# Batch 0's first-stage results moved inside SBUF, x laid out for 2 KB packets, and seven weight bands begun among batch 0's pairs

## The chip, the cores and the metric

The kernel runs on one core of one Trainium2 chip. The metric is the device time of one execution, in microseconds (us); the time before is 2643.61 us, the median of three runs (2640.65 to 2645.09 us). A profile of one further execution goes with it.

## The reference

`reference` has two halves. The first takes x (8 batches, 3008 positions, 256 channels), does a real FFT along the positions, multiplies each frequency by a complex 256x256 matrix, adds a bias, shrinks both parts towards zero by 0.01, and transforms back. The second is a feed-forward layer on the 24064 rows that result.

```python
X = np.fft.rfft(x, axis=1)
Yr = Xr @ w_r - Xi @ w_i + b_r
Yi = Xr @ w_i + Xi @ w_r + b_i
Yr = np.sign(Yr) * np.maximum(np.abs(Yr) - lam, 0.0)   # Yi likewise, lam = 0.01
y = np.fft.irfft(Y, n=x.shape[1], axis=1)
h = y.reshape(-1, 256) @ moe_w_in        # 256 x 2048, given in float64
g = h * np.clip(h + 3.0, 0.0, 6.0) / 6.0
return g @ moe_w_out                      # 2048 x 256, float64
```

## The kernel before

**The transform.** 3008 is 64 times 47, so a transform of one batch is a transform of length 47 (`stage1`), one of length 64 (`s2` in `middle`), the complex matrix and the shrinking (`s3`), one of length 64 back (`s5`), and one of length 47 back (`segment`). Between them the data change from one arrangement over the partitions to another, and they do so by way of DRAM: `scr1` between `stage1` and `s2`, `scr2` between `s5` and `segment`.

**Stage 1 of batch 0** handles seven sets of the 64 rows n1: one of four rows (96 partitions) and six of ten (120 partitions). For each set and for each of two results (c = 0, 1), TensorE makes one product into PSUM (L295), ScalarE copies it to a tile `a` (L303), and ScalarE's DMA queue stores it to `scr1` (L305, `scr<-a`). A partition of `a` is one pair (n1, k); `s2` wants n1 and c on the partitions and k in the free dimension. So `middle(0)` loads, for each of twelve pairs g of k, 128 partitions x 2 KB of `scr1` (L367, `bt<-scr`) and a piece of the table f64 (L368, `f<-in_f`).

**The pairs of batch 0.** `s2(g)`: eight products (L376); ScalarE and VectorE split the result into a high and a low part, the tile `X` (L130 and L131). `s3(g)`: 24 products of `X` with the matrices (L137, into `ps_a`), then VectorE adds the bias and shrinks (L414, L425, L426), ScalarE multiplies signs (L429), and copies of 64 partitions (`zt<-tc`, DMA L439, or VectorE L437 for the last two pairs) turn the tile. `s5(g)`: two products (L453), a copy (L455), a store to `scr2` (L456). Then two segments are loaded (`qt<-scr`), transformed (L505) and joined (`raw`, L515 and L527), and `prepare(0)` makes the seven split operands `yb` of the first 512 rows.

**The weight bands.** The weights of the second half come as float64. Each is cut into eight bands (`in_band`, `out_band`), and a band is decoded on the chip: one load of 512 KB (L178, `st<-in_w_in` or `st<-in_w_out`); then on VectorE L190, L191, L195, L199; on ScalarE L193, L194, L197; on GpSimd L200 and, for an `in` band, four sums (L217); and then the split into a high part by ScalarE and a low part by VectorE (`w_in_lo`, `w_out_lo`). An `in` band has seven instructions on VectorE (three for the low part), an `out` band five: 96 for all sixteen bands. `turn` begins a band and moves those begun a step on. Among batch 0's pairs it begins one at steps 0, 3, 9, 18 and 27 of 36 (`EARLY`, which uses the buffers `raw` and `yb`); after them and in the main loop it begins the rest (`LATE`, other buffers).

**The main loop** goes through 47 chunks of 512 rows and eight bands each: products with `w_in` (`pb`, `pc`, `pd`, L137), the gate (L608, L610, and a split `gs`), products with `w_out` (L631). The transforms of batches 1 to 7 are laid among them.

**What sets the order.** The code gives an order, and a scheduler moves an instruction ahead when it holds its buffers and inputs to be there. On the chip each engine, and each engine's DMA queue, takes its instructions in the order that results. Every DMA counts on one of eight semaphores, in turn, and waits until the DMA eight before it (the one before on that semaphore) has landed; the queues of SyncE (SP) and ScalarE share the eight.

## Time and profile before

| what | value |
|---|---|
| median of three runs | 2643.61 us |
| profiled execution, its own time | 2643.59 us |
| its span | 2641.8 us |
| TensorE busy | 2562.4 us (97%) |
| VectorE busy | 1975.7 us (75%) |
| ScalarE busy | 1820.1 us (69%) |
| granted TensorE clock, mean | 0.988 |

The span is the time from the first to the last instruction of the profiled execution; the 1.8 us between it and that execution's time lie around it. A busy share is a mean over stages of very different kinds: the first 135 us hold the transform of batch 0 and most of the decoding of weights, and what follows is the main loop. The stages are therefore read from a table of stretches, not from the page's shares.

### The profile page before, as it was taken

How to read it: one execution, taken by the hardware profiler on the slowest of the kernel's cores; microseconds unless marked ns; L12 is line 12 of the kernel's file. 1: busy time of each engine (PE TensorE's matmuls, PEld its weight loads, DVE VectorE, ACT ScalarE, POOL GpSimd, SP SyncE). 2: the span in 40 equal slices, each digit the busy share in tenths (PEclk: the TensorE clock that was granted, in tenths of full speed). 3: DMA queues.
4: the chain of work that ended last, by engine and by line, in shares of the span. 5: the costliest groups of instructions: out<-in, count | busy, mean ns of one | idle time of the engine just before them, and what ended most of it. 6: DMA issues, size and time to landing. Idle time of an engine off the chain costs nothing.

```text
span 2641.8 us, 44527 instructions
## 1 busy us (share of the span) xinstructions
PE 2562.4 (97%) x16406; PEld 2291.9 (87%) x16406; DVE 1975.7 (75%) x3186; ACT 1820.1 (69%) x3592; POOL 796.0 (30%) x749
## 2 busy tenths in 40 slices
PE   5789999999999999999999999999999999999999
PEld 3577998988898998988898998999889889898887
DVE  7786886877677777777777777777777777666766
ACT  5476677767667777766776777677777666676766
POOL 2263334443233332233323333233321121121210
PEclk8889999999999999999999999999999999999999
DMA  7623333332223321323213322233221111100000
GB/s 216 191 79 93 103 104 94 113 107 75 59 60 96 88 69 48 85 78 90 73 49 86 88 76 63 76 84 84 63 79 58 50 53 53 43 26 30 12 17 17
DMA packets 150178, 199.98 MB, mean 76 GB/s; under 512 B 16847, under 2 KB 104135, under 8 KB 149959
## 3 DMA queue, kind: packets, MB, share of 16 engines
q1 hardware_dynamic: 146675, 193.98, 25.4%
q10 hardware_dynamic: 3284, 3.15, 0.4%
q8 instruction: 129, 2.11, 0.3%
q14 instruction: 90, 0.74, 0.1%
HBM read 97.45 MB, written 74.97 MB: 65 GB/s over the span
## 4 chain that ended last, share of the span: by engine, by line
PE 84%; DVE 4%; ACT 4%; DMA 2%; POOL 2%; issue 2%; SPq 0%; ACTq 0%; POOLq 0%; DVEq 0%
PE po L631 36%; PE pb L137 17%; PE ps_a L137 11%; PE pc L137 9%; PE pd L137 4%; PE ps_a L505 3%; PE ps_a L376 3%; ACT gs L130 1%; DMA xin<-in_x 1%; DVE r L610 1%; ACT r L608 1%; DVE gs L131 1%; POOL e L288 1%; DVE h L572 1%; POOL yb L131 0%
## 5 line engine op out<-in xcount | busy, mean ns | idle before, releaser
L631 PE MATMUL po<-gs,w_out_hi 128*128 128x512 f32 x3008 | 1006.5, 396 | 0.0
L610 DVE SCALAR_TENSOR_TENSOR r<-r,h 128x1024 f32<-128x1024 f32 x376 | 486.9, 1295 | 267.7 <-ACT r L608 265.9
L631 PEld LDWEIGHTS po<-gs,w_out_hi 128*128 128x128 f32 x3008 | 541.3, 188 | 85.5
L631 PE MATMUL po<-gs,w_out_lo 128*128 128x512 f32 x1504 | 601.9, 400 | 5.9 <-ACT gs L130 3.3
L608 ACT ACTIVATE r<-h,three 128x1024 f32<-128x1024 f32 x376 | 434.3, 1155 | 214.6 <-DVE h L572 211.6
L137 PE MATMUL pb<-yb,w_in_hi 128*128 128x256 f32 x3008 | 571.6, 279 | 2.5 <-POOL yb L131 2.5
L131 DVE TENSOR_TENSOR gs<-r,gs 128x1024 fp32r<-128x1024 f32 x376 | 484.4, 1288 | 80.7 <-ACT gs L130 78.8
L137 PEld LDWEIGHTS pb<-yb,w_in_hi 128*128 128x128 f32 x3008 | 461.0, 189 | 22.5 <-POOL yb L131 2.7
L130 ACT CAST gs<-r 128x1024 fp32r<-128x1024 f32 x376 | 395.8, 1053 | 92.5 <-DVE r L610 89.5
L572 DVE TENSOR_TENSOR h<-pc,u 128x256 f32<-128x256 f32 x752 | 315.1, 419 | 175.3 <-PE pc L137 160.1
L131 POOL TENSOR_TENSOR yb<-T,yb 128x256 fp32r<-128x256 f32 x188 | 181.0, 969 | 859.4 <-ACT yb L130 841.6
L137 PE MATMUL pb<-yb,w_in_lo 128*128 128x256 f32 x1504 | 431.3, 288 | 4.6 <-ACT p L567 1.6
L567 ACT COPY u<-pb 128x256 f32<-128x256 f32 x752 | 277.8, 373 | 121.5 <-PE pb L137 103.8
L631 PEld LDWEIGHTS po<-gs,w_out_lo 128*128 128x128 f32 x1504 | 284.0, 189 | 63.3 <-ACT gs L130 14.5
L137 PEld LDWEIGHTS pb<-yb,w_in_lo 128*128 128x128 f32 x1504 | 284.3, 189 | 29.7 <-ACT h L601 4.1
L137 PE MATMUL pc<-yb,w_in_hi 128*128 128x256 f32 x1504 | 297.6, 279 | 0.8 <-POOL yb L131 0.8
L137 PEld LDWEIGHTS pc<-yb,w_in_hi 128*128 128x128 f32 x1504 | 230.7, 189 | 13.3 <-POOL yb L131 1.1
L137 PE MATMUL pc<-yb,w_in_lo 128*128 128x256 f32 x752 | 219.0, 291 | 5.5 <-DVE h L572 4.9
L567 ACT COPY p<-pb 128x256 f32<-128x256 f32 x376 | 139.9, 372 | 80.9 <-PE pb L137 78.6
L601 ACT COPY h<-pb 128x256 f32<-128x256 f32 x376 | 140.5, 374 | 57.4 <-PE pb L137 55.4
L572 DVE TENSOR_TENSOR h<-pd,p 128x256 f32<-128x256 f32 x376 | 156.7, 417 | 14.9 <-ACT p L567 10.2
L137 PEld LDWEIGHTS pc<-yb,w_in_lo 128*128 128x128 f32 x752 | 142.1, 189 | 21.7 <-DVE h L572 7.9
(125 smaller groups left out, 3928.9 us busy)
## 6 DMA issues: line engine op xcount, KB each, us to landing
bt<-scr SPq DMA_DIRECT2D x96, 256.0 KB, 2.9
scr<-pt SPq DMA_DIRECT2D x96, 256.0 KB, 2.4
zt<-tc SPq DMA_DIRECT2D x376, 64.0 KB, 2.0
out<-ot SPq DMA_DIRECT2D x94, 256.0 KB, 2.3
xin<-in_x SPq DMA_DIRECT2D x48, 480.0 KB, 4.8
qt<-scr SPq DMA_DIRECT2D x96, 240.0 KB, 3.5
scr<-a SPq DMA_DIRECT2D x84, 240.0 KB, 2.5
f<-in_f SPq DMA_DIRECT2D x96, 128.0 KB, 2.8
```

The source lines that it names most:

```text
L130: nc.scalar.copy(out=hi, in_=src)
L131: (on or nc.vector).tensor_tensor(out=lo, in0=src, in1=hi.bitcast(F32), op=ALU.subtract)
L137: nc.tensor.matmul(out=ps, lhsT=a, rhs=b, start=start and n == 0, stop=stop and n == len(todo) - 1, skip_group_check=more,)
L288: (nc.vector if b == 0 else nc.gpsimd).tensor_tensor(out=e, in0=plus, in1=minus, op=ALU.add)
L376: nc.tensor.matmul(out=psv[:, dh, :, u, :], lhsT=data[:, u, dh * P : (dh + 1) * P], rhs=f[:, u, :], start=True, stop=True,)
L505: nc.tensor.matmul(out=ps[:, cs * w + g * rows : cs * w + (g + 1) * rows], lhsT=qt[:rows, cs, g, dh * P : (dh + 1) * P], rhs=f47_s[2][:row ...
L567: nc.scalar.copy(out=t, in_=ps)
L572: nc.vector.tensor_tensor(out=to, in0=ps, in1=keep.pop((i, n)), op=ALU.add)
L601: nc.scalar.copy(out=hs[i][:, 1, :H], in_=pb)
L608: nc.scalar.activation(out=r, in_=h, func=AF.Relu, bias=three, scale=1.0)
L610: nc.vector.scalar_tensor_tensor(out=r, in0=r, scalar=6.0, in1=h, op0=ALU.min, op1=ALU.mult)
L631: nc.tensor.matmul(out=pos[dh], lhsT=w[:, ft * D + dh * P : ft * D + (dh + 1) * P], rhs=g[:, low, u], start=f == 0 and u == 0 and which == ...
```

## The change

It has three parts.

1. **Batch 0's stage-1 results stay in SBUF.** The two tiles `w_in_hi` and `w_in_lo` become one tile of sixteen slots: slot f is the high part of band f, and slot 15 - f its low part. Slots 4 to 10 (the high parts of bands 4 to 7 and the low parts of 5 to 7) also serve as `spread`, a view of 24 x 256 floats per partition, until the bands are written there. Instead of a store to `scr1` and twelve loads, each tile `a` is copied by DMA from 120 partitions x 1 KB to five partitions x 24 KB of `spread`, one copy per half of the tile (`g`): the first half by ScalarE's queue, the second by SP's. There are 26 such copies (the small set has one half). `s2` reads `spread` directly; the twelve loads `bt<-scr` of batch 0 are gone. Batches 1 to 7 keep `scr1`.
2. **x is laid out on the host as two rows of sixteen blocks** per partition, so that a load of a set has two runs of 2 KB per partition where it had one of 4 KB (for the small set two of 1 KB for one of 2 KB).
3. **`EARLY` bands** are begun at steps 0, 3, 9, 15, 21, 27 and 33: seven.

```diff
-    win_s = [const.tile([P, nf, 7, P], F32R, name="w_in_" + t) for t in ("hi", "lo")]
+    win_t = const.tile([P, 2 * nf, 7, P], F32R, name="w_in")
+    win_s = [[win_t[:, f] for f in range(nf)], [win_t[:, 2 * nf - 1 - f] for f in range(nf)]]
+    spread = win_t[:, nf // 2 : nf // 2 + 7].rearrange("p f s c -> p (f s c)").bitcast(F32)
+    spread = spread[:, : NK * D].rearrange("p (k d) -> p k d", d=D)
...
-            at = n1 // J * 2 * D
-            src = x[b, :rows, at : at + 2 * w].rearrange("p (s c) -> p s c", s=2)
+            at = n1 // J * D
+            src = x[b, :rows].rearrange("p (s c) -> p s c", s=2)[:, :, at : at + w]
...
-                dst = scr1[b][c, n1 : n1 + n].rearrange("(g j) k d -> (j k) g d", g=w // D)
-                (nc.sync if b else nc.scalar).dma_start(out=dst, in_=a.rearrange("p (g d) -> p g d", d=D))
+                if b:
+                    dst = scr1[b][c, n1 : n1 + n].rearrange("(g j) k d -> (j k) g d", g=w // D)
+                    nc.sync.dma_start(out=dst, in_=a.rearrange("p (g d) -> p g d", d=D))
+                else:
+                    for g in range(w // D):
+                        at = c * N1 + n1 + g * J
+                        queue = nc.sync if g else nc.scalar
+                        queue.dma_start(out=spread[at : at + rows // NK], in_=a[:, g * D : (g + 1) * D])
...
-            bt[g] = space([P, 2, D], F32, "bt"), space([P, 2, P], F32, "f64")
-            nc.sync.dma_start(out=bt[g][0], in_=src[:, 2 * g : 2 * g + 2, :])
+            bt[g] = space([P, 2, D], F32, "bt") if b else spread[:, 2 * g : 2 * g + 2], space([P, 2, P], F32, "f64")
+            if b:
+                nc.sync.dma_start(out=bt[g][0], in_=src[:, 2 * g : 2 * g + 2, :])
...
-            turn(EARLY if i == 3 or i % 9 == 0 else None)
+            turn(EARLY if i == 0 or i % 6 == 3 else None)
```

What this does to the order of the instructions shows at three places. In the rows below, a name is that of a tile with its number mostly left out, `w_in<-a` is a copy into `spread`, and the line numbers after the change are a few higher.

SP's queue at the end of stage 1, where the tables and the first bands are loaded. Before:

```order
L151 DMA g_all<-in_g 128x128
L368 DMA f_232<-in_f 128x256
L368 DMA f_236<-in_f 128x256
L178 DMA st<-in_w_in 128x2x512 x4
L178 DMA st<-in_w_out 128x1024
L367 DMA bt<-scr_95 128x512 x2
```

After:

```order
L151 DMA g_all<-in_g 128x128
L315 DMA w_in<-a 5x24x256 x3
L379 DMA f_241<-in_f 128x256
L315 DMA w_in<-a 5x24x256 x4
L379 DMA f_243<-in_f 128x256
L181 DMA st<-in_w_in 128x2x512
L315 DMA w_in<-a 5x24x256 x2
L181 DMA st<-in_w_in 128x2x512 x2
L181 DMA st<-in_w_out 128x1024 x2
```

Twelve copies into `spread` (nine of them here) now stand in this queue, and ten of the twelve stand ahead of the first band's load.

VectorE up to the split of the first pair (`X<-pb,X`). Before, the last rows ahead of it:

```order
L131 TENSOR_TENSOR w_in_lo<-m,w_in_hi 128x256
L131 TENSOR_TENSOR w_in_lo<-m,w_in_hi 128x128
L195 SCALAR_TENSOR_TENSOR e<-st,e 128x512
L190 TENSOR_SCALAR e<-st 128x512
L191 TENSOR_SCALAR m<-st 128x512
L199 SCALAR_TENSOR_TENSOR m<-m,r 128x512
L131 TENSOR_TENSOR X<-pb,X 128x2x256
```

After, all rows from the first instruction on a band:

```order
L193 TENSOR_SCALAR e<-st 128x512
L194 TENSOR_SCALAR m<-st 128x512
L198 SCALAR_TENSOR_TENSOR e<-st,e 128x512
L202 SCALAR_TENSOR_TENSOR m<-m,r 128x512
L193 TENSOR_SCALAR e<-st 128x512
L194 TENSOR_SCALAR m<-st 128x512
L131 TENSOR_TENSOR X<-pb,X 128x2x256
```

Before, 23 of the 96 band instructions of VectorE stand ahead of this split; after, six.

VectorE among the later pairs, from the seventh split. Before, up to the eighth:

```order
L131 TENSOR_TENSOR X<-pb,X 128x2x256
L414 TENSOR_TENSOR tc<-ps_a,bias 128x512
L425 TENSOR_SCALAR tc<-tc 128x512
L426 TENSOR_TENSOR tc<-tc 128x512
L131 TENSOR_TENSOR X<-pb,X 128x2x256
```

After, where the next row is the eighth split:

```order
L131 TENSOR_TENSOR X<-pb,X 128x2x256
L437 TENSOR_TENSOR tc<-tc 128x512
L198 SCALAR_TENSOR_TENSOR e<-st,e 128x512
L131 TENSOR_TENSOR w_in<-m,w_in 128x256
L131 TENSOR_TENSOR w_in<-m,w_in 128x128
L202 SCALAR_TENSOR_TENSOR m<-m,r 128x512
L425 TENSOR_TENSOR tc<-ps_a,bias 128x512
L131 TENSOR_TENSOR w_in<-e,w_in 128x512
L436 TENSOR_SCALAR tc<-tc 128x512
L437 TENSOR_TENSOR tc<-tc 128x512
L131 TENSOR_TENSOR w_out_lo<-m,w_out_hi 128x512
L425 TENSOR_TENSOR tc<-ps_a,bias 128x512
```

Between the first split and the twelfth and last stand 20 band instructions before and 54 after. From there to the last `zt` copies there are 10 before and 6 after, from these to the first sum of the main loop (`h<-pd`) 28 and 22, and later 15 and 8.

More of the change, by code (lines that the diff above doesn't have):

```diff
@@ L218, in in_band @@
         yield
-        hi, lo = (t[:, f] for t in win_s)
+        hi, lo = (t[f] for t in win_s)
         split(hi[:, :2], lo[:, :2], w[:, :, :P])
@@ L264, in stage1 @@
     def stage1(b):
-        scr1[b] = dram.tile([2, N1, NK, D], F32, name="scr1")
+        if b:
+            scr1[b] = dram.tile([2, N1, NK, D], F32, name="scr1")
         sets = SEGS[-1:] + SEGS[:-1]
@@ L354, in middle @@
         scr2[b] = dram.tile([2, N1, NK, D], F32, name="scr2")
-        src = scr1[b].rearrange("c n k d -> (c n) k d")
+        src = scr1[b].rearrange("c n k d -> (c n) k d") if b else None
         dst = scr2[b].rearrange("c n k d -> (c n) k d")
@@ L365, in load @@
         def load(g):
-            bt[g] = space([P, 2, D], F32, "bt"), space([P, 2, P], F32, "f64")
-            nc.sync.dma_start(out=bt[g][0], in_=src[:, 2 * g : 2 * g + 2, :])
+            bt[g] = space([P, 2, D], F32, "bt") if b else spread[:, 2 * g : 2 * g + 2], space([P, 2, P], F32, "f64")
+            if b:
+                nc.sync.dma_start(out=bt[g][0], in_=src[:, 2 * g : 2 * g + 2, :])
             nc.sync.dma_start(out=bt[g][1], in_=f64.rearrange("p (k c) -> p k c", c=P)[:, 2 * g : 2 * g + 2])
@@ L561, in block @@
         c, f = units[i]
-        product(ps, [(tuple(t[:, f, WEIGHT[n]] for t in win_s), yb[c, n])], start=start, more=True)
+        product(ps, [(tuple(t[f][:, WEIGHT[n]] for t in win_s), yb[c, n])], start=start, more=True)
     def kept(i, n, ps):
@@ L759 @@
     half = half.reshape(B, 2, 13, R47, D).transpose(0, 3, 2, 1, 4)
-    pairs = half[:, :, :12].reshape(B, R47, 6, 2, 2, D).transpose(0, 1, 2, 4, 3, 5)
-    xp = np.zeros((B, R47, 32 * D), np.float32)
-    xp[:, :, : 24 * D] = pairs.reshape(B, R47, 24 * D)
-    xp[:, :, 24 * D : 26 * D] = half[:, :, 12].reshape(B, R47, 2 * D)
+    xp = np.zeros((B, R47, 2, 16, D), np.float32)
+    xp[:, :, :, :13] = half.transpose(0, 1, 3, 2, 4)
+    xp = xp.reshape(B, R47, 32 * D)
     pos = positions()
```

## The prediction

> **What bounds the kernel now.** I read the page first, for where TensorE (PE) is not busy.
>
> ```profile
> span 2641.8 us, 44527 instructions
> PE   5789999999999999999999999999999999999999
> ```
>
> A digit is 66 us. Only the first three are under 9, so the main loop is bound by TensorE, and this change, which touches batch 0's transform, can only move its start and its first hundred microseconds. Then a table of stretches, cut where the stages of batch 0 end:
>
> ```profile
> core 0: us, PE busy (x) PEld busy (x) DVE busy (x) ACT busy (x) POOL busy (x), PEclk, DMA share, GB/s
> 27.50:41.40 13.90, 1.57 (x4) 0.28 (x2) 9.06 (x16) 10.10 (x19) 4.13 (x6) 0.73 0.90 298
> 49.30:60.00 10.70, 10.02 (x69) 10.02 (x70) 10.70 (x18) 6.29 (x13) 5.76 (x7) 0.77 0.31 108
> 60.00:80.00 20.00, 18.22 (x137) 16.41 (x136) 15.86 (x29) 10.11 (x19) 3.07 (x2) 1.00 0.50 139
> 80.00:101.20 21.20, 19.77 (x143) 17.22 (x141) 10.49 (x17) 7.08 (x14) 0.00 (x0) 1.00 0.69 203
> 101.20:117.00 15.80, 8.14 (x49) 5.87 (x47) 13.38 (x26) 9.65 (x18) 4.15 (x5) 0.85 0.73 226
> 117.00:126.20 9.20, 2.02 (x2) 0.45 (x2) 9.02 (x14) 6.21 (x12) 5.70 (x7) 0.50 0.48 146
> 126.20:135.50 9.30, 7.21 (x32) 6.96 (x32) 8.89 (x16) 5.07 (x12) 6.32 (x9) 0.50 0.70 180
> 135.50:200.00 64.50, 55.72 (x305) 47.92 (x304) 50.67 (x78) 45.96 (x95) 38.92 (x35) 0.89 0.30 81
> 200.00:260.00 60.00, 54.66 (x322) 47.28 (x322) 41.56 (x62) 40.12 (x80) 19.75 (x21) 0.97 0.30 82
> ```
>
> VectorE (DVE) is full from 49 to 60 us, has 4.1 us free to 80 and 10.7 us free to 101 (TensorE bounds there), and is full again from 117 to 135.5, where the main loop starts. Last, the timeline from stage 1 to the first and the last pair:
>
> ```profile
> 17.76 1.55 SPq L368 DMA_DIRECT2D f<-in_f  x2
> 19.43 13.75 SPq L178 DMA_DIRECT2D st<-in_w_in  x4
> 31.07 0.59 ACT L303 COPY a<-pb 120x512 f32<-120x512 f32 x1
> 37.23 0.81 SPq L367 DMA_DIRECT2D bt<-scr  x2
> 41.45 3.75 PE L376 MATMUL pb<-f,bt 128*128 128x128 f32 x16 [12.30 <-ACT m L197]
> 45.55 0.57 ACT L130 CAST X<-pb 128x512 fp32r<-128x512 f32 x1
> 49.25 0.68 DVE L131 TENSOR_TENSOR X<-pb,X 128x512 fp32r<-128x512 f32 x1
> 101.23 0.69 DVE L131 TENSOR_TENSOR X<-pb,X 128x512 fp32r<-128x512 f32 x1 [0.53 <-ACT X L130]
> ```
>
> The last `a` is copied at 31.66 us. Through DRAM it reaches the first products 9.8 us later; their split waits on until 49.25, because VectorE has decodes ahead of it. The twelfth split comes 52.0 us after the first. These two splits are my marks.
>
> **The round trip and its replacement.** Stores and loads through `scr1` go; 26 copies inside SBUF come, the same 3,072 packets of 1 KB as the stores had. What a packet costs, and on how many DMA engines a copy runs, comes from three stretches: 20 to 41 us (the stores, on ScalarE's queue q10), 5 us of the main loop with only four `zt` copies of 64 partitions, and 3.4 us with only one store of 120 partitions.
>
> ```profile
> q10 hardware_dynamic: 2943, 2.83, 39.7%
> ...
> DMA packets 320, 0.26 MB, mean 52 GB/s; under 512 B 64, under 2 KB 320, under 8 KB 320
> q1 hardware_dynamic: 320, 0.26, 22.0%
> zt<-tc SPq DMA_DIRECT2D x4, 64.0 KB, 2.0
> ...
> DMA packets 255, 0.25 MB, mean 72 GB/s; under 512 B 15, under 2 KB 255, under 8 KB 255
> scr<-a SPq DMA_DIRECT2D x1, 240.0 KB, 2.5
> ```
>
> Stores: 39.7% of 16 engines x 21 us over 2,943 packets is 45.3 ns. The `zt` copies stay inside SBUF: 22.0% of 16 x 5 us is 17.6 us, over 256 packets of 1 KB some 67 ns (the 64 tiny ones counted in). The tiny packets (under 512 B) are each engine's mark that it is done: 64 for four `zt` copies are 16 engines each, 15 for the store of 120 partitions are 15. So an engine took four or eight whole partitions; no row shows one partition shared between engines. A copy into five partitions therefore runs on five engines at the least (one each), on 15 at the most (by the source's 120).
>
> I take five. Each then carries 3,072 / 5 = 614 packets: 27.8 us at 45.3 ns, 41.1 us at 67 ns, against 9.3 us on 15 engines. The eight semaphores let only the small copies and about two more go before SP's queue has seen x land (17.76 us). The other 22 of 26 need 23.5 to 34.8 us. On the same engines run one band and two table pieces (512 and 2 x 128 KB, 48 KB per engine, 2.2 us at 45.3 ns per KB), and the last copy lands up to 2.0 us after its issue (the `zt` row). So the data are there at 45.5 to 56.8 us. One of the two pairs' products (half of 3.75 us), the cast and the split add 3.1 us, and only six band instructions stand ahead of the split. The first split comes at 48 to 60 us; I take the middle, 54: **+4.8 us**. On 15 engines the last copy would land as the stores did, 5.1 us after 31.66 (the issue view of 20 to 41 us), the split at 40: -9.2 us.
>
> ```profile
> scr<-a ACTq DMA_DIRECT2D x11, 240.0 KB, 5.1
> ```
>
> The Trainium skill ("DMA: Bandwidth & Descriptors", section "Why a DMA increments its semaphore by 16 and not by 1") says that a copy runs on the largest number up to 16 that divides the outermost dimension of both sides. That agrees with the 16 and the 15 above and gives five here, four for the small set; by it the sum is the one I take.
>
> **The bands.** Their loads stand behind ten copies in SP's queue, so VectorE, which decodes from 27.5 us now (9.06 us of work to 41.4), mostly idles until about 45. What it has not decoded moves among the pairs: 34 more band instructions between my marks (54 for 20). Their price, from the groups up to 140 us:
>
> ```profile
> L131 DVE TENSOR_TENSOR w_in_lo<-m,w_in_hi 128x256 fp32r<-128x256 f32 (+1 forms) x14 | 11.4, 845 | 0.0
> L195 DVE SCALAR_TENSOR_TENSOR e<-st,e 128x512 int32<-128x512 int32 x14 | 10.7, 767 | 1.9 <-ACT e L194 1.9
> L191 DVE TENSOR_SCALAR m<-st 128x512 int32<-128x512 int32 x14 | 8.3, 606 | 0.6 <-POOL e L217 0.4 <-DMA zt<-tc 0.2
> L190 DVE TENSOR_SCALAR e<-st 128x512 int32<-128x512 int32 x14 | 8.1, 582 | 3.8 <-DMA st<-in_w_in 2.0 <-DMA st<-in_w_out 1.8
> L199 DVE SCALAR_TENSOR_TENSOR m<-m 128x512 f32<-128x512 int32 x6 | 5.9, 990 | 0.0
> L199 DVE SCALAR_TENSOR_TENSOR m<-m,r 128x512 f32<-128x512 int32 x7 | 5.5, 784 | 0.2
> L131 DVE TENSOR_TENSOR w_in_lo<-e,w_in_hi 128x512 fp32r<-128x512 f32 x7 | 5.5, 781 | 0.0
> L131 DVE TENSOR_TENSOR w_out_lo<-m,w_out_hi 128x512 fp32r<-128x512 f32 x5 | 3.4, 680 | 0.0
> ```
>
> 58.8 us over 81 instructions: 0.726 us each. Between the marks VectorE is busy 10.70 + 15.86 + 10.49 = 37.1 us of 52.0; 34 x 0.726 = 24.7 us more make 61.8, more than the stretch holds: **+9.8 us**, with VectorE in TensorE's place as the bound. At the cheapest full-width price (582 ns) it is +4.9; with 4 us of idle time left over, +14.
>
> What was put forward is missing later. To 117 us four fewer, 2.9 us of 13.38 busy in 15.8: **-2.9**. To 135.5 six fewer, 4.4 us. VectorE is full there (17.9 of 18.5), but beside it runs a chain by way of `scr2`, whose load alone held TensorE 7.2 us:
>
> ```profile
> PE ps_a L505 <- DMA qt<-scr: 7.2, 1, 7.2
> ```
>
> I take **-2.5**, bounds 0 and -4.4. In the main loop seven fewer, 5.1 us, where TensorE has 8.8 + 5.3 us idle to 260 us and VectorE is three quarters busy: **-2**, bounds 0 and -5.
>
> **What I cost at nothing.** The twelve loads `bt`: two pairs ahead of use, TensorE's 4.4 us a pair (10.02 + 18.22 + 19.77 over eleven) covers them; with no cover each would cost its 4.2 us (37.23 to 41.45). x in twice the packets: the same bytes; the copies on five engines end later than x, which hides either sign, and later batches load x a set ahead under a bound TensorE. Writing bands 4 to 7 over `spread`: the scheduler puts these after the pairs that read there; if one comes early, what queues behind it is the next `X`, one pair, 4.4 us.
>
> **Sum.** +4.8 + 9.8 - 2.9 - 2.5 - 2 = +7.2 us. The profiled execution took 2643.59 us, 1.8 more than its span and equal to the median, so I say **2651 us**. What this kernel's measurement can tell from no change is about 0.2%, 5.3 us. With the arrival at its ends (-0.7, +10.6) the case's own range is 2645 to 2657.
>
> **Rivals.**
>
> *The copies run on 15 engines* (faster). For: a store of the same tile shows 15. Against: they would have to share a destination partition. -9.2 in place of +4.8 gives -6.8: 2637. Chance 0.25.
>
> *VectorE absorbs it* (no change). For: 14.9 us free between the marks, and decode prices that fall when GpSimd is out of the way (784 for 990 ns in L199's two forms). With the +4.9 price, and the later gains at their bounds (-2.9, -4.4, -5), the sum is -2.6; with half of these it is +3.6: about 2644. Chance 0.20.
>
> *Five neighbouring partitions jam* (much slower). 64 partitions written by 16 engines cost 67 ns where 45 was free. If four engines meeting at one place cost twice that again, 134 ns, a copying engine needs 82 us, 22/26 of it 70: the data come at 92 us, the split at 95, +46 + 2.4 (the other four terms): about 2692. It decides from some 80 ns a packet on. Against: copies from two queues go to different partitions at once, and engines drift apart. Chance 0.10.
> The Trainium skill ("SBUF — State Buffer", section "Door 1: The DMA port swizzle") says that four neighbouring partitions share one port; that agrees with 67 for 45 ns.
>
> **How the numbers follow.** Forecast 0.45, 15 engines 0.25, absorbed 0.20, jam 0.10. Of the forecast's own range, 2645 to 2657, a third lies within +5.3, and a tenth of the absorbed case beyond -5.3. Slower: 0.10 + 0.32 (seven tenths of 0.45) = 0.42. Faster: 0.25 + 0.02 = 0.27. The same: 0.13 + 0.18 = 0.31. The range reaches to 2634 below (15 engines with a little more) and to 2665 above (the forecast with more idle time), and leaves out the jam and the far end of the 15 engines.
>
> **What would show it.** Five tiny packets per copy, not 15. The first products at 45 to 57 us and VectorE idle before them: right; at 37: 15 engines; after 75: the jam. The twelfth split about 62 us after the first with VectorE full: right; 52: absorbed. If TensorE runs its pairs at 4.4 us with the new decodes beside it, the second term is wrong; if the main loop starts before 135 us, the whole is.

## The result and the profile after

The change made the kernel slower: 2674.54 us, median of four runs (2673.6 to 2675.63), against 2644.35 (2640.65 to 2645.44) for the kernel before. The ratio is 1.0117, 95% interval 1.0099 to 1.0134. The sign was predicted, the size was not: +7 was forecast, +30 came, and 2674.5 lies above the range's end at 2665. The profiled execution took 2674.54 us, its span is 2672.4, at a mean granted clock of 0.984 (0.988 before).

The page after, TensorE's row in 40 slices (67 us each):

```profile
span 2672.4 us, 44526 instructions
...
PE   3879999999999999999999999999999999999999
```

Where before had 5, 7 and 8 it has 3, 8 and 7: the loss begins in the first slice. The table of stretches, cut at the marks of the prediction (first split, twelfth split, last `zt` copy, start of the main loop) and at the 13th output store. The columns are length, then busy time and instructions of TensorE, its weight loads, VectorE, ScalarE and GpSimd, then granted clock, DMA share and GB/s. Before:

```profile
49.25:101.23 51.98, 48.04 (x344) 43.66 (x345) 37.10 (x63) 23.56 (x45) 8.83 (x9) 0.95 0.53 159
101.23:116.80 15.57, 8.09 (x48) 5.81 (x46) 13.21 (x25) 9.42 (x18) 3.95 (x5) 0.85 0.74 228
116.80:135.50 18.70, 9.25 (x34) 7.46 (x34) 18.07 (x30) 11.48 (x24) 12.22 (x15) 0.50 0.59 162
135.50:581.40 445.90, 428.73 (x2721) 383.41 (x2721) 347.05 (x547) 314.12 (x639) 183.04 (x159) 0.98 0.34 97
581.40:2641.80 2060.40, 2046.31 (x13220) 1841.51 (x13219) 1530.49 (x2479) 1437.45 (x2825) 576.38 (x544) 1.00 0.22 63
```

After:

```profile
66.80:129.20 62.40, 51.37 (x342) 45.77 (x342) 57.24 (x95) 39.54 (x74) 22.94 (x25) 0.91 0.48 141
129.20:144.00 14.80, 8.71 (x55) 6.60 (x53) 12.90 (x24) 7.34 (x14) 5.87 (x8) 0.96 0.58 182
144.00:160.90 16.90, 9.22 (x34) 7.42 (x35) 10.14 (x22) 10.62 (x21) 4.68 (x7) 0.50 0.55 169
160.90:607.50 446.60, 429.76 (x2716) 381.91 (x2716) 343.50 (x538) 308.84 (x631) 168.65 (x158) 0.98 0.34 96
607.50:2672.40 2064.90, 2048.81 (x13227) 1842.35 (x13225) 1536.32 (x2480) 1437.74 (x2826) 573.27 (x544) 1.00 0.22 63
```

The rows give the difference stage by stage; the first mark itself moved from 49.25 to 66.8 us.

| stretch | predicted | measured |
|---|---|---|
| to the first split | +4.8 | +17.6 |
| first to twelfth split | +9.8 | +10.4 |
| to the last `zt` copy | -2.9 | -0.8 |
| to the main loop | -2.5 | -1.8 |
| main loop to the 13th store | -2 (with the next) | +0.7 |
| from there to the end | | +4.5 |
| sum | +7.2 | +30.6 |

So two things went wrong: the copies arrive late, far beyond the term's own range (-0.7 to +10.6), and the main loop gives 5.2 us more instead of 2 less. The timeline after shows the first (start, length, engine, line; in brackets the idle time ahead, and what ended it):

```profile
18.76 0.82 SPq L315 DMA_DIRECT2D w_in<-a  x1
...
35.88 10.01 SPq L315 DMA_DIRECT2D w_in<-a  x4
...
47.26 0.63 SPq L181 DMA_DIRECT2D st<-in_w_in  x1
...
50.42 4.34 SPq L315 DMA_DIRECT2D w_in<-a  x2
...
59.89 0.43 DVE L193 TENSOR_SCALAR e<-st 128x512 int32<-128x512 int32 x1 [11.60 <-DMA st<-in_w_in]
...
64.11 3.12 PE L387 MATMUL pb<-f,w_in 128*128 128x128 f32 x13 [26.23 <-DMA st<-in_w_out]
...
66.81 0.69 DVE L131 TENSOR_TENSOR X<-pb,X 128x512 fp32r<-128x512 f32 x1 [0.39 <-ACT X L130]
```

SP's queue issues its first copy at 18.76 us (the prediction had 17.76) and its last two between 50 and 55. In between it waits seven times for an earlier copy to land, as each DMA does for the one eight before it (its waits from 15 to 60 us: total, times, longest):

```profile
SPq L315 <- DMA w_in<-a: 16.9, 7, 3.6
```

The first band's load, behind ten of these copies, is issued at 47.26 (19.43 before), and VectorE stands idle for it until 59.89. TensorE idles 26.2 us in one piece. The row puts that down to a band's load; that band is no input of the product, so it was another DMA: of the product's inputs the last to be sent is `spread`, whose last copy is issued at 54.0 us.

### The profile page after: what moved, and what is told of

Read it like the earlier page. It is cut to its first block, busy times and chain, and to the rows that moved or that the text cites. A ratio compares the mean times of both kernels' runs of the same rounds, so it can differ in the third digit from the quotient of the medians.

```text
span 2672.4 us, 44526 instructions
## 1 busy us (share of the span) xinstructions
PE 2570.9 (96%) x16406; PEld 2293.9 (86%) x16406; DVE 1977.5 (74%) x3186; ACT 1819.3 (68%) x3592; POOL 778.9 (29%) x749
## 2 busy tenths in 40 slices
DMA packets 154125, 196.83 MB, mean 74 GB/s; under 512 B 16571, under 2 KB 103859, under 8 KB 153907
## 4 chain that ended last, share of the span: by engine, by line
PE 80%; DVE 5%; ACT 4%; DMA 2%; issue 2%; POOL 1%; SPq 0%; ACTq 0%; DVEq 0%; POOLq 0%
PE po L642 35%; PE pb L137 17%; PE ps_a L137 10%; PE pc L137 9%; PE pd L137 4%; PE ps_a L516 3%; PE ps_a L387 3%; ACT gs L130 2%; DVE r L621 2%; DMA xin<-in_x 1%; ACT r L619 1%; DVE gs L131 1%; DVE h L583 1%; POOL e L292 0%; DVE tc L437 0%
## 5 line engine op out<-in xcount | busy, mean ns | idle before, releaser
L137 PE MATMUL pb<-yb,w_in 128*128 128x256 f32 x4512 | 703.4, 282 | 7.7 <-POOL yb L131 3.8
L137 PEld LDWEIGHTS pb<-yb,w_in 128*128 128x128 f32 x4512 | 630.5, 189 | 53.2 <-POOL yb L131 4.3
L137 PE MATMUL pc<-yb,w_in 128*128 128x256 f32 x2256 | 394.2, 283 | 3.3 <-DVE h L583 2.6
L137 PEld LDWEIGHTS pc<-yb,w_in 128*128 128x128 f32 x2256 | 336.1, 189 | 31.9 <-DVE h L583 6.3
L137 PE MATMUL pd<-yb,w_in 128*128 128x256 f32 x1128 | 198.3, 283 | 2.0 <-DVE h L583 1.9
L137 PEld LDWEIGHTS pd<-yb,w_in 128*128 128x128 f32 x1128 | 165.0, 189 | 12.2 <-DVE h L583 4.3
L292 POOL TENSOR_TENSOR e<-xin 120x512 f32<-120x512 f32 (+1 forms) x49 | 66.4, 1354 | 278.5 <-DMA xin<-in_x 278.5
L131 POOL TENSOR_TENSOR xs<-xin,xs 120x512 fp32r<-120x512 f32 (+1 forms) x42 | 55.0, 1310 | 309.2 <-ACT xs L130 259.4
```

The lines of the kernel that those rows point to most:

```text
L131: (on or nc.vector).tensor_tensor(out=lo, in0=src, in1=hi.bitcast(F32), op=ALU.subtract)
L137: nc.tensor.matmul(out=ps, lhsT=a, rhs=b, start=start and n == 0, stop=stop and n == len(todo) - 1, skip_group_check=more,)
L292: (nc.vector if b == 0 else nc.gpsimd).tensor_tensor(out=e, in0=plus, in1=minus, op=ALU.add)
```

## The experiments

All times are medians in us; ratios are to the kernel before on the same chip. "First split" and "main loop" are the marks in each kernel's trace.

| kernel | stage-1 results | x | bands | time | ratio, 95% | first split | twelfth | main loop |
|---|---|---|---|---|---|---|---|---|
| before | DRAM | 4 KB | five | 2644.35 | 1 | 49.2 | 101.2 | 135.5 |
| stores_on_five | DRAM, 26 stores | 4 KB | five | 2645.42 | 1.0010 (1.0001-1.0019) | 44.2 | 98.2 | 133.5 |
| seven_alone | DRAM | 4 KB | seven | 2650.26 | 1.0030 (1.0019-1.0041) | 48.2 | 106.4 | 141.7 |
| x2k_alone | DRAM | 2 KB | five | 2651.18 | 1.0025 (1.0013-1.0036) | 45.6 | 101.1 | 134.7 |
| x2k_and_seven | DRAM | 2 KB | seven | 2661.08 | 1.0062 (1.0047-1.0077) | 47.5 | 110.4 | 144.8 |
| move_alone | neighbours | 4 KB | five | 2674.28 | 1.0126 (1.0109-1.0143) | 67.4 | 130.4 | 165.7 |
| x_4k | neighbours | 4 KB | seven | 2663.0 | 1.0075 (1.0058-1.0092) | 66.9 | 126.3 | 161.8 |
| five_bands | neighbours | 2 KB | five | 2672.05 | 1.0110 (1.0095-1.0126) | 65.6 | 124.0 | 160.1 |
| the change | neighbours | 2 KB | seven | 2674.54 | 1.0117 (1.0099-1.0134) | 66.8 | 129.2 | 160.9 |
| x2k_first_batch | neighbours | batch 0 2 KB, later 4 KB | seven | 2668.39 | 1.0103 (1.0088-1.0118) | 66.8 | 129.1 | 159.7 |
| x2k_later_batches | neighbours | batch 0 4 KB, later 2 KB | seven | 2679.34 | 1.0144 (1.0129-1.0159) | 67.4 | 126.4 | 161.3 |
| apart_13_x4k_five | 13 apart | 4 KB | five | 2660.1 | 1.0065 (1.0050-1.0080) | 55.3 | 118.0 | 152.7 |
| apart_13_x4k | 13 apart | 4 KB | seven | 2650.03 | 1.0028 (1.0017-1.0038) | 55.5 | 114.6 | 149.9 |
| apart_13 | 13 apart | 2 KB | seven | 2665.14 | 1.0089 (1.0072-1.0106) | 54.9 | 118.8 | 150.0 |
| gpsimd_queue | neighbours | 2 KB | seven | 2711.76 | 1.0262 (1.0245-1.0279) | 108.4 | 162.9 | 193.1 |

The marks of x2k_alone are those of x2k_again, the same kernel once more.

### On how many engines the copies run

No run is needed for this. The page's packet rows, of before and of after; the prediction read the count under 512 B as the engines' marks, one per engine and transfer:

```profile
DMA packets 150178, 199.98 MB, mean 76 GB/s; under 512 B 16847, under 2 KB 104135, under 8 KB 149959
```

```profile
DMA packets 154125, 196.83 MB, mean 74 GB/s; under 512 B 16571, under 2 KB 103859, under 8 KB 153907
```

Gone are twelve stores of 120 partitions (15 marks each), two of 96 (16 each) and twelve loads of 128 (16 each): 180 + 32 + 192 = 404. With five engines for each of the 24 copies into five partitions and four for each of the two into four, 128 come: 276 fewer in all. 16847 - 16571 is 276. The copies ran on five engines, and the rival of 15 is out.

### Do neighbouring partitions jam? (apart_13)

The same 26 copies, but to partitions 13 apart; the rows of one table are put in the matching order.

```diff
-                        at = c * N1 + n1 + g * J
+                        at = c * N1 + n1 // J + g
-                        queue.dma_start(out=spread[at : at + rows // NK], in_=a[:, g * D : (g + 1) * D])
+                        end = at + 13 * (rows // NK - 1) + 1
+                        queue.dma_start(out=spread[at:end:13], in_=a[:, g * D : (g + 1) * D])
```

> The changed kernel with the five partitions of a copy 13 apart instead of side by side (the rows of batch 0's f64 table are permuted to match); the order of the instructions is the same. Theory (five engines, and their writes meet at neighbouring partitions, which makes a 1 KB packet 60 ns and more instead of 46): packets at 46 to 50 ns, the first split 7 to 10 us sooner, 2664 to 2668 us. Rival (the number of engines alone): packets as in the change, 2672 to 2677 us.

Measured: 2665.14 us (1.0089, 1.0072 to 1.0106), 9 us less than the change, as the theory had it. A stretch of each in which the copies run, the DMA share in 40 slices and ScalarE's queue, which holds copies alone (packets, MB, share of 16 engines). The change, 30 to 46 us:

```profile
DMA  2233333333333334933333333233333332333333
...
q10 hardware_dynamic: 689, 0.68, 15.5%
```

apart_13, 25 to 36 us:

```profile
DMA  3333333333333333368633333333333333333333
...
q10 hardware_dynamic: 642, 0.63, 16.6%
```

And the twelve splits of apart_13 (shortest, median and longest in ns, first and last start):

```profile
L135 DVE TENSOR_TENSOR X<-pb,X x12: 677/680/691, 54.9 to 118.8; 128x512 fp32r<-128x512 f32 x12
```

A digit of 3 is five engines of 16; both kernels keep five busy, but a packet takes 15.5% x 16 x 16 us / 689 = 57.6 ns with neighbours and 16.6% x 16 x 11 us / 642 = 45.5 ns with 13 between. The 45.5 is what the stores to DRAM had (45.3). The price depends somewhat on the stretch; over 15 to 62 us, which holds nearly all the copies, the same queue has, in the change and in apart_13:

```profile
q10 hardware_dynamic: 1648, 1.62, 13.6%
...
q10 hardware_dynamic: 1638, 1.61, 10.5%
```

These are 62 and 48 ns. For the 614 packets of an engine that is 38 against 30 us, some 8.5 of the 11.9 us by which the first split comes earlier; 1.9 more are that SP's first copy is issued at 16.87 and not 18.76, and the remaining 1.5 I don't assign. The Trainium skill ("SBUF — State Buffer", section "Door 1: The DMA port swizzle (why `[64,N]` ≈ `[32,N]`)") has four neighbouring partitions on one port; the direction agrees. The size is for the run to say: 27 to 29% per packet, not the 134 ns that the rival "jam" put there.

The same edit was made beside 4 KB packets of x, with seven bands (below) and with five: the first split moves from 66.9 to 55.5 and from 67.4 to 55.3, the ratio by -0.47% and -0.61% (here -0.28%). Three times some 12 us at the mark, 7 to 16 us at the end.

### Another queue for the copies (gpsimd_queue)

```diff
-                        queue = nc.sync if g else nc.scalar
+                        queue = nc.gpsimd
```

> The changed kernel with all 26 copies issued from GpSimd's queue instead of ScalarE's and SP's. Theory (it is the same five DMA engines for every copy that cost): if copies from this queue take other engines in turn, the first split comes at 45 us or sooner and the time is 2636 to 2650 us; if they stay on five, 2660 us or more. Rival (the copies' number and their semaphores hold the stage up, whatever the engines): the first split at 60 us or later and 2668 us or more.

Measured: 2711.76 us (1.0262, 1.0245 to 1.0279). This lies within the rival's bounds and also within the theory's second case (2660 or more), so it doesn't tell them apart; neither foresaw a first split at 108 us. Of its page, all packets and GpSimd's queue; of 20 to 100 us, the same queue and the landing (median us); of the timeline, TensorE's first product:

```profile
DMA packets 153836, 196.85 MB, mean 73 GB/s; under 512 B 18587, under 2 KB 102803, under 8 KB 153619
q0 software_dynamic: 2912, 3.18, 0.8%
```

```profile
q0 software_dynamic: 2684, 2.98, 24.8%
...
w_in<-a POOLq DMA_DIRECT2D x23, 120.0 KB, 5.9
```

```profile
101.40 3.75 PE L387 MATMUL pb<-f,w_in 128*128 128x128 f32 x16 [67.61 <-DMA w_in<-a]
```

SP's queue was freed, and the first decode came at 32.4 us where the change has 59.9. But 23 copies took 80 us, 3.5 each. The packets are of another kind, too: against the change's page 3,072 fewer lie between 512 B and 2 KB, 768 more between 2 and 8 KB, and 2,016 more under 512 B, so the 3,072 KB went in packets of 4 KB. A price per packet therefore can't be compared; per KB of the queue, 24.8% x 16 x 80 us over 2.98 MB (2,910 KB) is 109 ns, where ScalarE's queue in the change has 65 (1.62 MB, 15 to 62 us). The run tells nothing of what the early bands alone are worth. A later arrival does carry to the end here: the first split is 41.6 us later, the main loop 32 us, the time 37 us.

### The same 26 transfers to DRAM (stores_on_five)

The kernel before, its stores cut into halves and put on both queues as the copies are. The edit was meant to confine them to five engines.

```diff
+                    for g in range(w // D):
+                        at = n1 + g * J
+                        queue = nc.sync if g else nc.scalar
+                        queue.dma_start(out=scr1[b][c, at : at + rows // NK], in_=a[:, g * D : (g + 1) * D])
```

> The kernel before, with batch 0's stage-1 stores to DRAM cut as the copies are (26, from 120 partitions to five rows, on both queues); the loads and five bands as before. Theory (five engines set the arrival): packets at 45 ns, 28 us of stores, the first pair's products at 52 to 58 us instead of 41, and 2650 to 2662 us. Rival (the move inside SBUF is what costs): 2642 to 2648 us.

Measured: 2645.42 us (1.0010, 1.0001 to 1.0019), the first split at 44.2 us. But the edit did not do what was meant:

```profile
DMA packets 150358, 199.98 MB, mean 76 GB/s; under 512 B 17027, under 2 KB 104315, under 8 KB 150139
```

17027 - 16847 + 212 = 392 = 24 x 15 + 2 x 16: the halves went on 15 and 16 engines; as I read it, because five rows of `scr1` lie in one piece and the 120 packets can be dealt out. So the numbers that look like the rival's aren't its confirmation. The run is a control: nearly twice as many transfers, on both queues and waiting for each other, cost 0.10% (0.01 to 0.19; and bring the first split 5 us earlier). What costs is where they go, and with it on how many engines they run; this run doesn't part the two.

### The other two parts, alone and together (seven_alone, x2k_alone, x2k_again, x2k_and_seven)

All three leave the results in DRAM. Seven bands:

```diff
-            turn(EARLY if i == 3 or i % 9 == 0 else None)
+            turn(EARLY if i == 0 or i % 6 == 3 else None)
```

> The kernel before with seven bands begun among the pairs, nothing else. 38 band instructions stand between the first and the twelfth split where 20 stood: 13 us more for VectorE, which has 14.9 us free there. Theory: they fit nearly, and what is gone later gives it back: 2638 to 2646 us. Rival (the bands fill VectorE and cost 10 us, as in the change): 2652 us or more.

x in packets of 2 KB (with the layout on the host that goes with it):

```diff
-            at = n1 // J * 2 * D
-            src = x[b, :rows, at : at + 2 * w].rearrange("p (s c) -> p s c", s=2)
+            at = n1 // J * D
+            src = x[b, :rows].rearrange("p (s c) -> p s c", s=2)[:, :, at : at + w]
```

> The kernel before with x in packets of 2 KB, nothing else. The scheduler then puts 34 band instructions between the first and the twelfth split where 20 stood. Theory: stage 1 ends at most 3 us later, and the 34 fit nearly: 2641 to 2649 us. Rival (x's packets cost): 2655 us or more.

> The kernel before with x in packets of 2 KB, taken once more for an undisturbed trace; 2650 to 2653. Theory: the cost lies in the main loop: from the 13th output store to the end 2064 to 2065 us, as in the four kernels with 2 KB packets, against 2059.4 to 2060.9 in the four with 4 KB, and the start of the main loop within 2 us of 135.5. Rival: the cost lies ahead of the main loop, in x's first seven sets that land later: then the main loop starts 4 us or more later, and the stretch behind the 13th store is 2060 to 2061 us.

And both edits:

> The change without its largest part: batch 0's stage-1 results go through DRAM as before, the other two parts (x in packets of 2 KB, seven bands among the pairs) stay. What is left to the change, 2674.5 less this time, is the price of the move within SBUF. Theory: the two small parts add (+6.6 and +7.5 alone): 2655 to 2660, the first split at 47 to 50 us, and the move itself costs 15 to 19 us. Rival: the small parts overlap, since a later start of the pairs hides in the same idle time: 2650 to 2653, and the move costs 22 us or more.

Measured: 2650.26 (1.0030), 2651.18 (1.0025) and, once more, 2649.32, and 2661.08 (1.0062); the last two kernels come out a microsecond or two above their theories. Together they cost as much as the two alone or a little more (0.62% against 0.55%, each known to some 0.1%), and more than half of what the whole change costs (1.17%). The splits of seven_alone:

```profile
L131 DVE TENSOR_TENSOR X<-pb,X x12: 675/678/693, 48.2 to 106.4; 128x512 fp32r<-128x512 f32 x12
```

38 band instructions of VectorE stand between these (20 before): 58.2 us for 52.0. The start of the pairs is hardly touched (48.2 us for 49.2); the bands' price lies among the pairs, and it is 6 us at the main loop's start and 0.30% of the time (8 us). Theory and rival had both missed it, one from each side.

x2k_again, in the main loop to the 13th store and from there on:

```profile
134.70:583.70 449.00, 428.74 (x2725) 382.80 (x2725) 346.09 (x539) 309.05 (x632) 177.20 (x159) 0.98 0.34 96
583.70:2647.40 2063.70, 2047.35 (x13217) 1840.36 (x13215) 1535.78 (x2480) 1439.64 (x2827) 572.50 (x544) 1.00 0.22 63
```

Here the main loop starts 0.8 us *earlier* than before; the 5.6 us of the span come in it, 3.1 to the 13th store and 3.3 behind (the theory had 2064 to 2065 for the last, and no part of it ahead). The cost of this edit is thus not in stage 1, where the prediction had looked for it and found it hidden.

### The change with one part undone (x_4k, five_bands) and the move alone

x_4k takes x's packets back to 4 KB, five_bands the number of bands to five (the edits above, reversed); move_alone has both.

> The changed kernel with x in its old layout (packets of 4 KB). Theory (copies on five engines): the first split comes at most 3 us sooner, at 64 us or later, and the time is 2668 to 2676 us. Rival (x's 2 KB packets delay stage 1): the first split at 55 us or sooner and 2660 us or less.

> The changed kernel with its bands begun at steps 0, 3, 9, 18 and 27 again (five, as before). Theory: the time is lost where the copies run on five DMA engines, so the first split of a pair stays at about 67 us; 47 band instructions instead of 54 stand between the first and the twelfth split (about 5 us less there), and 11 and 26 instead of 6 and 22 behind them (about 6.5 us more): 2671 to 2678 us, like the change. Rival (the two more bands among the pairs are what costs): 2660 us or less.

> Only the move within SBUF, as the change has it (neighbouring partitions); x in packets of 4 KB and five bands as before. Without the move the other two parts gave 2661, the whole change 2674.5: 13.5 us for the move. Theory: the move costs about the same alone, since the arrival of its copies does not depend on the other two: first split at 63 to 68 us, 2655 to 2663. Rival: five bands are the worse number once the bands come late, as they were with the copies 13 partitions apart (2660 with five, 2650 with seven): 2668 to 2676.

Measured: 2663.0, 2672.05 and 2674.28 us. The first split stays where the change has it, within 1.2 us, in all three: neither x nor the bands bring the copies in later. five_bands is as its theory had it. x_4k in three stretches (start, to the 13th store, rest):

```profile
0.00:161.80 161.80, 92.32 (x469) 69.72 (x469) 102.61 (x175) 73.29 (x140) 41.60 (x49) 0.77 0.56 155
161.80:597.50 435.70, 424.83 (x2716) 379.48 (x2715) 338.52 (x533) 307.96 (x627) 165.48 (x157) 0.99 0.35 97
597.50:2658.40 2060.90, 2046.55 (x13227) 1841.49 (x13225) 1530.90 (x2480) 1438.74 (x2827) 582.52 (x544) 1.00 0.22 63
```

Against the change, nothing to the main loop (161.8 for 160.9), 10.9 us less to the 13th store and 4.0 less behind it. The theory, which had put x's price at no more than 6 us, fell; so did the rival, which had the first split at 55 us or sooner. How much of the 14.9 us is the packets', the last runs below take up.

move_alone went against the theory too, and on the rival's side: without seven bands the move costs 33 us, as much as the whole change (1.26% and 1.17%; the intervals overlap). Its splits:

```profile
L131 DVE TENSOR_TENSOR X<-pb,X x12: 674/681/693, 67.4 to 130.4; 128x512 fp32r<-128x512 f32 x12
```

63.0 us from first to twelfth where x_4k, with more bands begun, takes 59.4. So an edit that costs 0.30% on the kernel before gains 0.51% when the results are moved (1.0126 to 1.0075) and 0.37% when they are moved 13 apart (1.0065 to 1.0028, below). Of the 12.8 us between the spans of move_alone and x_4k, 3.9 come by the main loop's start, 7.9 to the 13th store, where the two have the main loop's instructions in different orders, and 1.0 behind it. With x in 2 KB packets five bands and seven make no difference (1.0110 and 1.0117).

### Two repairs at once (apart_13_x4k, apart_13_x4k_five)

> The change with two edits at once: the copies go to partitions 13 apart (as in apart_13) and x keeps packets of 4 KB (as in x_4k). Alone they gave 2665 and 2663, against 2674.5 for the change. Theory: the two act in different places, the first in the arrival of the copies (first split at 66.8 before it, 54.9 with it), the second in the main loop, and their gains add: the first split at 52 to 57 us, and 2650 to 2656. Rival: both gains are the same few microseconds of an early stall that TensorE's queue of ready work makes up either way: then 2660 to 2665.

> Only the move within SBUF is left of the change, with its copies 13 partitions apart; x in packets of 4 KB and five bands as before. Theory: what stays is the copies on five engines at some 51 ns a packet (first split at 53 to 57 us for 49.2 before) and the bands that VectorE could not decode before the pairs, which the number of bands begun among the pairs does not change: 2649 to 2655. Rival: with the arrival mended, five bands leave VectorE less to do between the first and the twelfth split than seven, and it reaches the kernel before: 2640 to 2646.

Measured: 2650.03 us (1.0028, 1.0017 to 1.0038) and 2660.1 (1.0065, 1.0050 to 1.0080). The first is as the theory had it: the two gains add (0.28 and 0.42 from 1.17 leave 0.47; it is 0.28, so if anything they do more than add). With seven bands and 4 KB packets the move then costs nothing that can be told from zero (2650.03 against seven_alone's 2650.26), with a first split 7.3 us later than there. That zero is a sum: the main loop starts 8.2 us later than in seven_alone, the stretch to the 13th store is 9.8 us shorter (436.1 for 445.9), and the one behind it 2.7 longer. So the late arrival is not mended; another stretch, whose instructions stand in another order, makes up for it. The second is outside both theories, above them. Neither of the two is faster than the kernel before, and no kernel of this study is.

### Where the price of the 2 KB packets arises (x2k_first_batch, x2k_later_batches)

The change, with the 2 KB layout for batch 0 alone, and for batches 1 to 7 alone (`if not b` in the first line, which is that of x2k_first_batch):

```diff
+            if b:
+                at = n1 // J * 2 * D
+                src = x[b, :rows, at : at + 2 * w].rearrange("p (s c) -> p s c", s=2)
+            else:
                 at = n1 // J * D
                 src = x[b, :rows].rearrange("p (s c) -> p s c", s=2)[:, :, at : at + w]
```

> The change, but only batch 0's x comes in packets of 2 KB; the other batches' in 4 KB. With 2 KB throughout it took 2674.5, with 4 KB throughout 2663. Theory: the price of the 2 KB packets lies in the main loop's loads and the order that goes with them, not in batch 0's stage 1: 2661 to 2666, and from the 13th store to the end 2059 to 2061.5 us. Rival: it lies in x's first seven sets, which stand ahead of everything: 2670 to 2676.

> The change with batch 0's x in packets of 4 KB and the later batches' in 2 KB: the other half of x2k_first_batch. Theory (main loop): 2670 to 2676, and 2063.5 to 2065.5 us from the 13th store to the end. Rival (batch 0's stage 1): 2661 to 2666. Should both halves stay near 2663, or both near 2674, the price is in neither's packets but in the order that comes with them.

Measured: 2668.39 us (1.0103, 1.0088 to 1.0118) and 2679.34 (1.0144, 1.0129 to 1.0159). To the 13th store and the rest, x2k_first_batch:

```profile
159.70:607.30 447.60, 431.07 (x2719) 383.20 (x2720) 351.81 (x543) 309.81 (x633) 183.34 (x158) 0.98 0.34 96
607.30:2667.00 2059.70, 2045.70 (x13221) 1840.23 (x13219) 1530.44 (x2479) 1437.64 (x2825) 575.15 (x544) 1.00 0.22 63
```

x2k_later_batches:

```profile
161.30:611.90 450.60, 433.24 (x2721) 384.64 (x2721) 337.44 (x535) 306.69 (x628) 171.69 (x157) 0.98 0.33 94
611.90:2675.80 2063.90, 2047.27 (x13220) 1840.74 (x13219) 1534.86 (x2479) 1437.12 (x2825) 573.47 (x544) 1.00 0.22 63
```

The place behind the 13th store is as the theory had it, the sizes are not. There the price goes with the later batches' packets, 2059.7 and 2063.9 us. All kernels bear that out: seven with the later batches at 2 KB take 2063.7 to 2065.3 us there, eight with them at 4 KB 2059.4 to 2062.1.

The edits also let the scheduler lay the instructions of the main loop in another order, so the order has to be held fixed before a price is given to the packets. Behind the 13th store the traces hold such pairs. There before, stores_on_five, seven_alone and x2k_first_batch (4 KB) have the same instructions in the same order on every engine and in SP's queue as x2k_and_seven and x2k_later_batches (2 KB): 2059.4 to 2060.4 us against 2063.9 and 2065.3. With another common order, x_4k and apart_13_x4k (4 KB) take 2060.9 and 2062.1, the change and apart_13 (2 KB) 2064.9 and 2064.1. So these 2 to 6 us are shown to be the packets'.

To the main loop nothing happens in either run. But between the two lies a stretch that was 435.7 us in x_4k and is 447.6 and 450.6 here: both halves cost more in it than 2 KB throughout (446.6). Prices of packets would add; these don't. And x2k_first_batch moves no packet of 2 KB of x in this stretch, since batch 0's x is loaded ahead of it: its 11.9 us more than x_4k are not the price of packets. Here the orders differ. Kernels that have the same order in it agree within 1 us, whatever came ahead: the change and apart_13 446.6 and 445.7, x_4k and apart_13_x4k 435.7 and 436.1, move_alone and apart_13_x4k_five 443.6 and 444.2, x2k_and_seven and x2k_later_batches 449.7 and 450.6. TensorE has the same work (2716 to 2721 matmuls); what differs is its idle time (10.9 us in x_4k, 16.5 and 17.4 here) and the time of its matmuls at a slightly lower clock (0.99 and 0.98). So these 12 us go with the order, not with packets. Whether the packets have a share in x2k_later_batches' 15, no pair with equal order tells, and why x_4k's order is the shorter stays open.

## Why the prediction came out as it did

**The first split, +4.8, measured +17.6: the step that failed is the sum for the arrival of the copies.** Its form was right: five engines, 614 packets each, the band's load behind ten copies, VectorE idle ahead of it. "VectorE mostly idles until about 45" was until 59.9. Three of its terms were too small.

The first is the number of copies that were still to come. The prediction let four of the 26 go before x has landed and priced the other 22. At the issue of SP's first copy, 18.76 us, SP's queue had moved none of the 3,072 packets and ScalarE's this many, marks included:

```profile
q10 hardware_dynamic: 117, 0.12, 3.2%
```

The second is the price, 62 ns over the whole time, where the middle of 45.3 and 67 is 56. 614 packets at 62 ns are 38 us, some 37 of them after 18.76 us; the forecast's middle has 29. The third is what runs beside the copies. 18.76 and 37 make 55.8 us, but the first product starts at 64.11: 8 us more, for which the prediction had 4.2 (2.2 for one band and two table pieces, 2.0 for the landing). Ahead of the last copies a band's load was issued, and three more DMAs of 512 KB follow at once. The after's DMA share from 46 to 63 us, in 40 slices of 0.43 us:

```profile
DMA  3358339699974333333322337999999999999974
```

Five engines up to 49 us, a burst with the first band, five again, and from 56 us all sixteen: the last copies, issued until 55 us, land among the bands' loads.

With 13 partitions between the destinations the first split came at 54.9 us, next to the 54 of the forecast, but that is luck: at that kernel's 48 ns the prediction's sum gives 50.

ScalarE was held up, too, which the prediction had not seen. Its waits for copies up to 60 us, after (total, times, longest), and the rows at both of them:

```profile
ACT a L307 <- DMA w_in<-a: 14.9, 2, 7.7
...
19.28 4.36 ACTq L315 DMA_DIRECT2D w_in<-a  x2
23.68 0.58 ACT L307 COPY a<-pb 120x512 f32<-120x512 f32 x1 [7.14 <-DMA w_in<-a]
...
26.68 6.75 ACTq L315 DMA_DIRECT2D w_in<-a  x3
33.47 0.58 ACT L307 COPY a<-ps_a 120x512 f32<-120x512 f32 x1 [7.71 <-DMA w_in<-a]
```

Both times the next `a` is copied 0.04 us after ScalarE's own DMA issues end, and these take 4.4 and 6.8 us, since each waits for a DMA eight before it. Seven tiles `a` take turns, but they are not what is missing: the first of the two waits is ahead of the sixth `a`. The prediction read the last `a` from before, at 31.7 us, and had the copies run as from a full store. It now comes at 47.0. The eight semaphores were used for the start of the copies alone, not for what they hold up in ScalarE. What these waits add to the arrival, beside the engines' own time, the traces don't separate.

**First to twelfth split, +9.8, measured +10.4.** Right in size, and right that VectorE is the one waited for: of 11.0 us in which TensorE idles there (3.9 before), 8.1 are for VectorE's `X` and `tc`. The idle time is 7.1 of the 10.4 us; the other 3.3 are TensorE's own, 51.37 us for 342 matmuls where before has 48.04 for 344, at a granted clock of 0.91 for 0.95, which the term did not have. TensorE's waits in the 62.4 us after (total, times, longest):

```profile
PE ps_a L137 <- DVE X L131: 6.6, 4, 2.8
PE pb L387 <- ACT pt L466: 2.9, 2, 2.1
PE ps_a L137 <- DVE tc L425: 1.5, 1, 1.5
```

Two more errors hide in the size, one up and one down, so that it came out so close is in part luck. VectorE was busy 57.24 us where 61.8 was forecast: its busy time rose by 20.1 us, 0.59 for each of the 34 extra band instructions and not 0.726. And 5.2 us of idle time were left over, which the term took as zero. The runs warn against reading more into it: x2k_and_seven has 39 band instructions there and takes 62.9 us, x_4k has 50 and takes 59.4. Their number alone doesn't set this stretch; that their place among the pairs does as well is likely, but no run tests it.

**The later stretches, -2.9 and -2.5, measured -0.8 and -1.8.** The right sign, a third and two thirds of the size. VectorE's busy time to the main loop fell from 18.07 to 10.14 us, and the stretch only by 1.8: the chain by way of `scr2` holds it, as said. TensorE's longest wait there is the prediction's own line again, 7.2 us for `qt<-scr`.

**The main loop, -2, measured +5.2.** The wrong sign. The bands' absence may show (to the first output store 73.6 us, 80.5 before), but it is given back by the 13th, where the order of the instructions is another one, and 4.5 us more go behind that, where x_4k with the same order and packets of 4 KB takes 4.0 less.

**x in 2 KB packets, costed at nothing: wrong.** The cover named was the late copies, for stage 1, and a bound TensorE with loads a set ahead, for the later batches. The first held: the main loop's start doesn't move with x. The second did not: +0.25% alone and +0.42% beside the move. Of that, 2 to 6 us behind the 13th store are shown to be the packets' (0.1 to 0.2% of the time); the rest comes with another order of the main loop and isn't parted from it.

**The removed loads and the bands over `spread`, costed at nothing: nothing seen against it.** No wait of TensorE between the first and the twelfth split names them.

**The rivals.** 15 engines: out, by the marks. VectorE absorbs: out, 62.4 us between the splits. The jam: its mechanism was at work, at 57.6 ns and not 134, so the case as priced (2692) did not come, and its "point from which it decides", 80 ns, was set too high: 57.6 in place of 45.5 (62 and 48 over the whole time) already moves the end by 7 to 16 us.

**The sum.** Of the 23.4 us that the forecast lacked, 12.8 are the first split, 0.6 the stretch behind it, 2.8 gains after the twelfth split that did not come, and 7.2 the main loop. Of the last, some 4 are x's packets behind the 13th store; the rest is not assigned, since the order of the instructions ahead of that store is another one in each of the kernels compared.

## What to carry to other kernels

Before a DMA is turned from DRAM to SBUF, count the partitions at its destination: here a tile that went out on 15 engines came in on five, and on neighbouring partitions each packet cost some 28% more; spreading the destination was worth 7 to 16 us and needed only another order of a table's rows. A transfer that gets slower holds more than its reader: look at what its issues hold up on the engine that makes them and what stands behind it in its queue, and add their loads on the same engines to the sum. And cost a change in the layout of an input where that input is loaded for the rest of the run, not only where the change is made; parts of a change that is spread over a schedule don't add, so undo each one in its place as well as doing it alone. Before a difference is put down to an edit, compare the order of the instructions in the two traces: here an order that came along was worth 12 us, more than the packets that were under test.

## What the runs showed of the hardware that was not expected

A copy of 120 KB from GpSimd's queue took 3.5 us in a row of its kind, in packets of 4 KB and at 109 ns per KB, where ScalarE's queue took 65 ns per KB with the same destinations and packets of 1 KB. Five rows of a DRAM tile, which lie in one piece, were written by 15 engines, five partitions of SBUF by five: the marks are 392 and 128. The Trainium skill ("DMA: Bandwidth & Descriptors", section "Why a DMA increments its semaphore by 16 and not by 1") goes by the slowest dimension as the instruction carries it; that fits both, if the five rows are carried as one run of 120, which the trace doesn't tell.
